# One string that orders 4,292 steps: the order of a gated recurrence and an MLP replaced by another order of the same instructions

## The chip, the core and the metric

The kernel runs on 1 core of one Trainium2 chip. The metric is device microseconds of one execution; three timed runs of the kernel before gave 839.09, 840.26 and 841.7 us, median 840.26 us. The trace comes from one profiled execution, whose span from the first to the last instruction is 837.2 us.

## What is computed

```
# q, k, v, a_re, a_im: (B, H, S, D) = (4, 8, 768, 48), float32
mag   = sqrt(a_re**2 + a_im**2)
scale = minimum(mag, 0.999) / (mag + 1e-6)          # a complex gate of modulus < 1
for t in range(S):                                  # state S: D x D complex, per batch and head
    S = gate[t] * S + k[t] (outer) v[t]
    y[t] = q[t] @ Re(S)
x = y, heads side by side: (B*S, H*D) = (3072, 384)
h = x @ w_in                                        # w_in: 384 x 2048, float64
g = maximum(h, 0) + alpha * minimum(h, 0)
out = g @ w_out                                     # w_out: 2048 x 384, float64; out: 3072 x 384
```

## The kernel before, in words

**The gates** (`gates`, lines 223 to 435). The recurrence is not run token by token. A prefix product of the gates gives each token a magnitude (a product over powers of two, "decays") and a phase ("rotation"). The work is cut into nine pieces: batch 0 in three (1, 2 and 3 chunks of 128 tokens), each of the other batches in two of 3 chunks. A piece loads `a_re` and `a_im` (L248), computes on ScalarE and VectorE (L254 to L311), builds the decays (L319) and writes them to DRAM (`decs`, L324), multiplies up the phases (L339, L341; the small ones on GpSimd) and writes those to DRAM (`phs`, L432).

**The units** (`unit`, from L646). One unit is one chunk of 128 tokens of one batch with all 8 heads: 24 units. `loads` fetches its q and k (L578, L580), its phases (`PP`, L586) and decays (`T`, L593). VectorE turns q and k by the phases (L662, L664) and then doubles the reach of the products level by level (L718, six levels); between these, ScalarE copies (L741, L757) feed small TensorE matmuls (L679), whose results are masked into `A` (L700 on ScalarE, L703 on VectorE). Further matmuls transpose k (L786), make the state of the chunk (L798), and sum the output y (L818, L842). The state passes from a unit to the next of its batch (L827, L830 on VectorE). y goes to DRAM (L861).

**The weights** (`to_f32`, from L490). w_in and w_out come as float64 words, in 16 loads (L492) into three regions of one buffer. Three ScalarE instructions (L508, L510, L512), one on GpSimd (L516) and two on VectorE (L518, L520) make each piece float32.

**The MLP** (`all_mlp`, L927). The tokens are handled in 14 groups of one or two chunks: sizes 1, 1, ten of 2, 1, 1. Once the units of a group have written y, its x is loaded (L874). Then for each of 16 blocks of 128 features: three matmuls (L890), Relu on ScalarE (L897), the slope on VectorE (L899), and, one or two blocks later, the matmul that adds the block to the output (L909). Each L890 or L909 call shows as two MATMUL records in the trace.

**What sets the order.** Every part is a Python generator. Its `yield`s cut it into steps: what stands between two yields (usually one instruction on one of VectorE, ScalarE, GpSimd, or a burst of TensorE matmuls, or one DMA issue on SyncE's queue) is one step. `Plan.run` (L96) walks through a string, `ORDER`, and for each letter advances the generator of that letter by one step:

```
    def run(self, order):
        for c in order:
            next(self.tasks[self.LETTERS.index(c)], None)
```

The letters are: A to I the nine pieces of the gates; J the loads of the units; K the rows of v for three of the levels (`half_rows`, L561); L the loads of v (L602 to L628); M the loads of the weights; N and O the making of w_in and w_out; P to Z and a to m the 24 units; n the loads of x; o the MLP. So the string alone fixes the program order of all instructions, and with it the order on each engine, since each engine runs its own instructions in program order, waiting at the first one whose inputs or buffer are not there. All DMAs are issued from SyncE's one queue, in the same way. Steps of one letter stay in their own order; only how the letters are mixed is free. `Ring` (L76) is left over from the making of the order: its `put` (L81) holds only `pass` and issues nothing.

Of the kernel before, what the change touches and what calls it, by code (L numbers as in the profile page):

```python
# [27 lines left out]


ORDER = (  # L30
    "AAAAAAAAAAAAAAAAAAAAAAAAAAMMMAAMMJBBBBAMBJNNNNAAAAAAAAAAAAABABNANAAAAAABAAAABBABBNNAABBMBBABBNAAAABB"
    "BBBKBAAKKBJNABAKBAKAKAKAKOKNKJKKKKAAAAKOBBBANAABKABOMAABMAAAAABABAAABAAOOOOOOOBNNOOBBNOONNBNMNNNBJJB"
    "BBBBOPJPONPPPPPNMNPPOOPOOOPPCCLLMMMLLLLBLLJBCBBBPBBBBBBBJJBBBBBBBBBBBBBPPPPPPNOBCCCPCPPPBBNKCKKKKKCK"
    "LLKLBBBBBOBLLPPPPPPPPBBBBBBBPCCCCCLCBBNCCJBBBBPPPOBOOOOCPPPPBCMJDDCCNCCOCOCPCJCNCOOCJJJCOCONNNNCCCPD"
    "DKCQCCCCCDDNCLLLLCQDCCQCCCCCCCCCCCOQLNLPPPPPPMQMQQQQPPPPJQQLODDQQQODJJOJJJJJJQQQDDQCQCCDCCQDCQRKCOKL"
    "CLLLLLLKnRRRQRQRQQQQQQQQQQRQRQQRCCCCCQCQCRCNNNDDCDDoDQooDoooLLLoooQoDMoLQooCDDDCoRCoCoCDoooooNRoNNCo"
    "CoKNCCCCLLLRRRoooooLLLLLLDRLRRQQCCCCCCCRKKRMKCCRRoQCDooCQQQQRRoRRQCCoooooCoCoDDDRRRRRRRRRRoDoRJORoDR"
    "oDOOOOODRJJEJNDoooooLLDRRRRoRRRRDoSoOooSDSooDLoooJoLLooSSDSEoooSJooDooonoSSoDoSSDNNNSLLENoDoSSSoooLN"
    "DLooooSDooRSSSEJoJooOOoooooSSSoJLESoTESSSSLoLLLoTSJoooJSSSJooJSoJJooooSSSSSSooDESSEKTKESSESSSSSSDSoo"
    "UDUooTTTDoDTDoDDDDDDKooDDDDoooooooTDTTTLEoEToooELLTTTTTooooLoooJoJoTTooooEoUTTTTTTTTooooooUUTToUTTLT"  # L40
    "EELLLLLLLLDDDDDDEEEDDDDDDDDLoooDDDDDDoTooTTTTooTLnLLLEEoooEUULLLLLLLKoTooooooEoLUEoooLoToDDUoTDooDUo"
    "DDDDooooooooUEoEEUUoEEEDTToTTTTTooToUoUoUoooUooDUooooDooooUUUUUUUUUoooooDDDUoDooUoUUooooEUUUUUUoDoEo"
    "oEoEoooJUJUUUUUEUEJEEJJoooooEJEoEJooooEoEooEUooEooEoooooVoooooooJEoVooVoVoooooVFFJJJooooUVJVVVFoEEoE"
    "EooEoEEEEEEVEVEnooJJVVELEEEoooooooLVoWWVVooLoLoLLFFVoooVVoooVWoLoEoooLoEooVLoWEWWVWoVEoVVVVoEoWLWLWE"
    "WLooEoFLVVVEVLoooVJJoVEoooVEJEJJWEEEEEoEFVVVVVVoWWVVVWFFFooELELoEooWFFFFFoooooLoWWLLLLLLWLoEoooooLEo"
    "EEEEoEoELLLoWWVVVVVVVEWVWWooooEoEooooJJEJooWoXWWWEFJWWEooooooWWoooooWWWWWWWWXWLLLWWWWWWWXFFooWoLLooL"
    "LXXXXoXooooXXXoJJJooooGXooooLXoFFFoGXXXXooooLXXooFoFooFoXYXoFXGonooooJJooLLGoYXXXooooXXXoXXoFLoLLFFF"
    "FYFooFoXYFoXoGYYYFYXYooFFooJJooFYoYooooooFKoJooJXXXXYXXLXXXXXGXXXXooFoXFooooFGoGooFFFFFFFFFFJJFJYYYY"
    "FooooYooYYooZoZZZoFooLoFLLLLooLLFLLFGLooooLooYYYYYLYLYoZYZZZZoooooKKKYKYooYooYooJooFFYFGKFFGZGJJGYYY"
    "YYYYYYYYLooLLoLFGKGoYYYYYYoZoKZoKooooooJoFLoFLFGoFGFFFoFFoFFFFFFFFFFoLLLZZZZnLZZZLooLLKooooLFFooooZo"  # L50
    "FZZooFFZFZFFoFoFJJFoJooFoFFooZZZJZJZoFZooooZZooZZZZZZZZZZZZFLLLFoaZZZZZaoooooooooooJaJJooaoGoooaaaaa"
    "ooooaoooooaoooGaaaaaaaaoooobooooGJGooLGoGGJGGaaaaaaaJJaLLLaGoGoooGoLLLLbbbbHHooooooaoooLoabLooaGGooG"
    "aaaaaaGaGaGHbbbHbGbHKbKGJaJaaooooooGGboooooooaoaaaGGaGoJoobbbboooGbbGbGGGGoGGGbcoooooooooLooLobLLLbL"
    "LLHJLbLJLcbLbboobooocoHobooooHHHooocobbbooocccccobbooLcnooLooooJJJHbbHHHbobbbbooLoHLLLHGccLLoLLLLLGL"
    "LHoGoooHoGooJGooHGboooooGoocGccGcGbGGGGbbGcGcGcGoooobobbobGJoooGGGGooGGGccccGGGGcoocccooLdccocoooodc"
    "ococccccccccccbbooJJLLGGGGGGGJJJGJcodcHcLLGococcHGGGoGoGooooooooLLoLoLoodooooodHGGdHoGodddddKKooHLLL"
    "LoKooHoooodoooddddJodLHLHoHddooJooHooHooddHooonodddHdoodddddooooHHHHHHHooooddIIoooodHHoddddJdddJddLH"
    "JdHdedddHHddeJJJoJJJJJJHooooooooooeooHoooooeeeeeeHeoeooooofooeooooofeeoeffeooeoooLLoooooJeoeooooooLe"
    "oeeeeeeffooogHHHHHHfHHHHHHHHHHHHHfHHHHHHHgHeeeeLLLLLLLLLLIKoooooeooeefeeeeeeeKeeeeeKeeeeHHooHooooofo"
    "ooJoHHHHfHJLLoLfoLHHLLLLoooLLooLffJJffIoILofLoLfofooooogoooogfgffffgfggfoffooooogggIoffooooooHHHHHHo"  # L60
    "HoooofIKooHHooofffffKKfngfHHofggggIIooKKLooooLLLLLLggLLLLgoLHoooggggggggoffffoffffooHofggfgoooooooHo"
    "ooooJJogooooLoooooIIgoooIJIIIIJoJgJJgggggggggohooIggggoIIoooooooIohhoogLLLLJJhhJJJoohoooooohhoooIooh"
    "hooohohoooohooonohoioIohhhhhohooiihoooooooooooJohiihiooIihIhhhIIIIhLoohooooKhoooohhLLoLLLLLILLIoIIIh"
    "oooiiihihhhhhhhhhhhhhhhhLoLhioooIooooooLLLLLooioiiioooiioioooIoooooiJiiiJooJJJLJJIIIIIIooooojoIoIooo"
    "ooIooIooojjIIIoIIIIoLIIoIIoIiijiiiiioooooooLojjLoLLoioLooioiIIIIiIIIIIIiIIIIIiiILLjLLLLLLLLojjjoioiI"
    "iioooojojooooojjioiIooIIiIIIIoILoojjjjojoooiILjjojiiioLLIIIIIIIIoIioooonjjjjjjjjooooIooIIooIooIooIoo"
    "oojooooojjjjjjjjjjjjjjjJJJJJjooooooojoooooJJJJoooookkLkoooooookoJooooookkoookkoookkoLojokokoookkkkko"
    "oJkoJJJJJkoooooookookkkkkkLLllLLoLLLLLoookkooLkLoooLkokookkkkkkkkkkkkkkklkokoooooooookLooooLllLllLLo"
    "nooooooololllJJloooooooJJooooooooLLoLollooomlollooolloooooooommmooooooomomolllolooooooommmmmoooLoLLL"
    "llllLooloooLmooommlmmoolloooooolollllllllllLlmllollloooooooooooooooooooomoooomoooooooooooooooooLLLLL"  # L70
    "LLooooooolooommmmmmoooooooooooomoooooooooooooomnoooooLLLLLooommmooooooomoommmmmmmmmmmmoooooooooomooo"
    "ommmoooooooooooonooooooooooooooooooooooooooooooooooooooooooooooooooooooooooooooooooooooooooooooooooo"
    "oooooooooooooooooooooooooooooooooooooooooooooooooooooooooooooooooooooooooooooooooooooooooooo")


# [26 lines left out]
def kernel(  # L102
# [83 lines left out]
    for h in (16, 32):  # L186
        by_row[h] = []
        for m in range(HC // h):
            t = next(column)
# [8 lines left out]
    def step(*args, **kwargs):  # L198
# [4 lines left out]
    R = {name: Ring(n) for name, n in dict(  # L203
        KQ=3, PP=1, T=2, V=1, WQ=2, W=1, run=1, St=3, xT=2, raw0=1, raw1=1, raw2=1, g0=0, g1=0, g2=0, ot=2, top=2,
        lv=2, misc=1, y=1, h=2, o=1).items()}
# [250 lines left out]
    def raw_done(name, f, e):  # L456

        i = 2 * f + (name == "out")
        for _ in range(6 if i >= NF - 3 else 1):
            R[("g" if i >= NF - 3 else "raw") + str(region(i))].put(e)  # L460
# [34 lines left out]
    def to_f32(dst, *key):  # L495

        n = 2 * DM
        ta = yield ACT(n + 100, ("raw", *key), takes=(R["top"],))
        raw = raws.pop(key)
        lo, hi = raw[:, :, :, 0], raw[:, :, :, 1]  # L500
        slot = slots.pop(0)
        top = tops[slot].rearrange("p (r e) -> p r e", r=dst.shape[1])
        top_u = top.bitcast(U32)

        def halfwords(z, dtype=U16):
            return z.rearrange("p r e -> p (r e)").bitcast(dtype)

        nc.scalar.activation(top, hi.bitcast(F32), AF.Abs)  # L508
        tl = yield ACT(n + 200)
        nc.scalar.activation(dst, lo, AF.Identity, scale=2.0 ** -51, bias=bias_two)  # L510
        tl = yield ACT(n + 100)
        nc.scalar.activation(halfwords(dst, BF16)[:, 1::2].rearrange("p (r e) -> p r e", r=dst.shape[1]), hi.bitcast(F32), AF.Sign, bias=bias_plus)  # L512
        raw_done(*key, tl)

        ta = yield POOL(1.4 * n, ta)
        nc.gpsimd.tensor_scalar(out=top, in0=top, scalar1=F64_SMALL, scalar2=None, op0=ALU.max)  # L516
        yield DVE(n // 2, ta)
        nc.vector.tensor_scalar(out=top_u, in0=top_u, scalar1=3, scalar2=None, op0=ALU.logical_shift_left)  # L518
        t = yield DVE(n, tl)
        nc.vector._custom_dve(ADD32_U16LIMBS, out=halfwords(dst), in0=halfwords(top), in1=halfwords(dst))  # L520
        slots.append(slot)
        return t

    def piece(dst, *key):
        if words:
            return (yield from to_f32(dst, *key))
        t = yield ACT(2 * DM, ("raw", *key))
        nc.scalar.copy(dst, raws[key])
        del raws[key]
        raw_done(*key, t)  # L530
        return t
# [470 lines left out]
```

## Time and profile before

| what | value |
| --- | --- |
| timed runs | 839.09, 840.26, 841.7 us |
| span of the profiled execution | 837.2 us |
| instructions | 26,824 |
| TensorE matmul busy | 696.3 us |
| VectorE (DVE) busy | 648.1 us |
| ScalarE (ACT) busy | 440.9 us |
| GpSimd (POOL) busy | 245.1 us |
| moved by DMA | 130.91 MB |

The page gives the busy time of each engine, then the span cut into 40 equal slices of 20.9 us, in which each digit is the busy share of an engine in tenths (9 is 90% or more). PEclk is the clock that TensorE was granted, in tenths of full speed. A row of a table by stretches gives, for a stretch of the span in us, the busy time of each engine with its instructions in brackets, the granted clock, the busy share of the 16 DMA engines, and what they moved in GB/s. A row of the waits reads: who waited (engine, what it writes, line), for whom, the time in total, how often, and the longest.

### The profile page before, as it was taken

What the parts mean: (1) busy time and instruction counts of PE and PEld (TensorE: products, weight loads), DVE (VectorE), ACT (ScalarE), POOL (GpSimd) and SP (SyncE); (2) the same over time, 40 slices, a digit from 0 to 9 for tenths busy, and PEclk for the clock granted to TensorE, in tenths of its full rate; (3) what the DMA queues carried; (4) which work ended last, traced back from release to release, by engine and by line L of the source; (5) the groups of instructions that cost most, each with busy time, mean ns of one, the idle gap of its engine ahead of it and who ended that gap; (6) DMA issues with size and microseconds to landing.
All of it is one profiled execution on the core that took longest, in us unless ns stands there. A gap on an engine that the chain in (4) does not pass through costs nothing.

```text
span 837.2 us, 26824 instructions
## 1 busy us (share of the span) xinstructions
PE 696.3 (83%) x11488; PEld 528.6 (63%) x11488; DVE 648.1 (77%) x953; ACT 440.9 (53%) x941; POOL 245.1 (29%) x352
## 2 busy tenths in 40 slices
PE   0002317768899999998999999999999999999998
PEld 0001316656777777776777777767777777777776
DVE  5988998989898998978998898796877856642112
ACT  7868876557645847473656544655443424232211
POOL 5376678817216400240134313500004300000000
PEclk9999757889999999999999999999999999999999
DMA  7695994696379468558854689457635493412100
GB/s 207 202 274 171 262 266 120 201 218 169 79 218 235 112 176 247 125 150 212 240 142 119 154 241 220 115 130 175 165 113 123 116 228 78 103 33 54 30 20 10
DMA packets 194174, 130.91 MB, mean 156 GB/s; under 512 B 74120, under 2 KB 185864, under 8 KB 194056
## 3 DMA queue, kind: packets, MB, share of 16 engines
q1 hardware_dynamic: 194056, 129.20, 58.7%
q8 instruction: 90, 1.47, 0.7%
q14 instruction: 28, 0.23, 0.1%
HBM read 100.82 MB, written 35.71 MB: 163 GB/s over the span
## 4 chain that ended last, share of the span: by engine, by line
PE 68%; DVE 12%; DMA 8%; ACT 5%; issue 3%; POOL 2%; SPq 2%; DVEq 0%; ACTq 0%; POOLq 0%
PE ps_h L890 27%; PE ps_o L909 26%; PE ps_lv L679 4%; PE ps_y L818 4%; DVE KQ L718 3%; PE ps_kv L798 3%; DMA T<-decs 3%; PE ps_y L842 2%; PE ps_kt L786 2%; DMA phs<-gate 2%; DVE gate L339 1%; DMA V<-in_v_dram 1%; DMA KQ<-in_k_dram 1%; DVE gate L341 1%; DMA St<-in_v_dram 1%
## 5 line engine op out<-in xcount | busy, mean ns | idle before, releaser
L890 PE MATMUL ps_h<-xT,w_in_sb 128*128 128x256 f32 (+1 forms) x1344 | 301.2, 356 | 3.0 <-issue 2.4
L909 PE MATMUL ps_o<-w_out_sb,g_sb 128*128 128x384 f32 x768 | 294.6, 497 | 10.7 <-DVE g_sb L899 8.3
L890 PEld LDWEIGHTS ps_h<-xT,w_in_sb 128*128 128x128 f32 x1344 | 234.1, 193 | 74.0 <-issue 4.3
L899 DVE SCALAR_TENSOR_TENSOR g_sb<-g_sb,al,ps_h 128x256 f32<-128x256 f32 (+1 forms) x224 | 97.5, 438 | 112.8 <-ACT g_sb L897 112.1
L909 PEld LDWEIGHTS ps_o<-w_out_sb,g_sb 128*128 128x128 f32 x768 | 137.7, 191 | 63.4 <-DVE g_sb L899 10.8
L718 DVE TENSOR_TENSOR KQ<-KQ,T 96x1024 f32<-96x1024 f32 x120 | 151.4, 1263 | 30.4 <-PE ps_lv L679 21.4
L897 ACT ACTIVATE g_sb<-ps_h 128x256 f32<-128x256 f32 (+1 forms) x224 | 78.7, 352 | 181.8 <-PE ps_h L890 181.1
L679 PE MATMUL ps_lv<-WQ 96*32 96x32 f32 x2304 | 34.5, 203 | 71.4 <-DVE WQ L662 55.1
L679 PEld LDWEIGHTS ps_lv<-WQ 96*32 96x32 f32 x2304 | 26.6, 115 | 93.1 <-DVE WQ L662 54.7
L339 POOL TENSOR_TENSOR gate<-gate 128x72 f32<-128x72 f32 (+1 forms) x56 | 40.0, 714 | 129.4 <-ACT gate L369 125.6
L741 ACT COPY WQ<-KQ 96x1024 f32<-96x1024 f32 x48 | 50.0, 1042 | 31.0 <-DVE KQ L718 30.7
L856 ACT COPY T<-ps_y 48x256 f32<-48x256 f32 x96 | 30.6, 365 | 46.8 <-PE ps_y L842 46.2
L757 ACT COPY W<-KQ 96x512 f32<-96x512 f32 x48 | 30.6, 638 | 45.7 <-DVE KQ L718 35.5
L516 POOL TENSOR_SCALAR top<-top 128x768 f32<-128x768 f32 x16 | 39.3, 2461 | 25.1 <-ACT top L508 17.1
L339 DVE TENSOR_TENSOR gate<-gate 128x576 f32<-128x576 f32 (+3 forms) x70 | 45.7, 653 | 1.2
L319 POOL TENSOR_TENSOR gate<-gate 128x72 f32<-128x72 f32 (+5 forms) x24 | 22.3, 929 | 76.6 <-DVE gate L319 74.3
L818 PE MATMUL ps_y<-A,VL 64*48 64x64 f32 x2304 | 43.5, 228 | 1.0 <-DMA VL<-vsc 0.7
L427 DVE TENSOR_TENSOR gate<-gate 128x1152 f32<-128x1152 f32 (+2 forms) x36 | 42.8, 1219 | 1.6 <-POOL gate L412 1.5
L679 PE MATMUL ps_lv<-KQ,W 96*32 96x32 f32 x1536 | 24.6, 205 | 23.4 <-ACT W L757 23.3
L818 PEld LDWEIGHTS ps_y<-A,VL 64*48 64x48 f32 x2304 | 41.6, 129 | 1.6 <-DMA VL<-vsc 0.9
L700 ACT ACTIVATE A<-ps_lv,columns 128x64 f32<-128x64 f32 x144 | 36.5, 334 | 9.6 <-PE ps_lv L679 9.5
L703 DVE TENSOR_TENSOR A<-ps_lv,mask 128x256 f32<-128x256 f32 x96 | 36.8, 412 | 0.0
(105 smaller groups left out, 925.3 us busy)
## 6 DMA issues: line engine op xcount, KB each, us to landing
T<-decs SPq DMA_DIRECT2D x48, 384.0 KB
PP<-phs SPq DMA_DIRECT2D x24, 387.0 KB
KQ<-in_q_dram SPq DMA_DIRECT2D x48, 192.0 KB
decs<-gate SPq DMA_DIRECT2D x7, 1152.0 KB
phs<-gate SPq DMA_DIRECT2D x14, 576.0 KB
KQ<-in_k_dram SPq DMA_DIRECT2D x40, 192.0 KB
vsc<-in_v_dram SPq DMA_DIRECT2D x48, 144.0 KB
VL<-vsc SPq DMA_DIRECT2D x24, 288.0 KB
```

Of the source, the lines that this page charges most:

```text
L339: on(4 * k).tensor_tensor(out=m, in0=w[:, 1::-1].unsqueeze(2).to_broadcast([P, 2, 2, k]), in1=pairs_of(u), op=ALU.mult)
L427: TT(out=m[:, a], in0=U5[:, 1 + a], in1=turned(off3, o)[:, a].unsqueeze(1).unsqueeze(3).to_broadcast([P, L // 2, nb, 2]), op=ALU.mult)
L516: nc.gpsimd.tensor_scalar(out=top, in0=top, scalar1=F64_SMALL, scalar2=None, op0=ALU.max)
L679: nc.tensor.matmul(t[64 * i + j:64 * i + j + HC // 2, p], lhsT=keys(n, g), rhs=queries(n, g), start=True, stop=True)
L703: nc.vector.tensor_tensor(out=a.rearrange("p n (g t) -> p n g t", g=2), in0=t.unsqueeze(2).to_broadcast(whole), in1=masks[name].rearrange( ...
L718: nc.vector.tensor_tensor(out=x, in0=x if x0 is None else x0, in1=m, op=ALU.mult)
L741: nc.scalar.copy(z.rearrange("p i n t -> p i (n t)").rearrange("p i (m h) -> p m i h", h=h), bass.AP(tensor=KQ.tensor, offset=KQ.offset + ...
L818: nc.tensor.matmul(o, lhsT=Vp[h][64 * i:64 * i + 64, s, e_ * D:(e_ + 1) * D], rhs=a, start=False, stop=False)
L890: nc.tensor.matmul(p, lhsT=w_in_sb[:, f // 2, kk, f % 2 * P:(f % 2 + 1) * P], rhs=x_of[m][:, kk], start=(kk == 0), stop=(kk == NK - 1))
L897: nc.scalar.activation(gt, p, AF.Relu, scale=-1.0)
L899: nc.vector.scalar_tensor_tensor(out=gt, in0=gt, scalar=al_1[:, f:f + 1], in1=p, op0=ALU.mult, op1=ALU.add)
L909: nc.tensor.matmul(sums[0], lhsT=gt[:, c * P:(c + 1) * P], rhs=w_out_sb[:, f], start=(f == 0), stop=(f == NF - 1))
```

## The change

The string is replaced by another one of the same length. Each letter occurs as often in the new string as in the old one, 1,552 times for the MLP, 49 times for most units. Besides, a line is added in `to_f32` that calls the empty `put`. The string has 43 lines; the first seven and the last two that differ are shown of each.

```diff
 ORDER = (
-    "AAAAAAAAAAAAAAAAAAAAAAAAAAMMMAAMMJBBBBAMBJNNNNAAAAAAAAAAAAABABNANAAAAAABAAAABBABBNNAABBMBBABBNAAAABB"
-    "BBBKBAAKKBJNABAKBAKAKAKAKOKNKJKKKKAAAAKOBBBANAABKABOMAABMAAAAABABAAABAAOOOOOOOBNNOOBBNOONNBNMNNNBJJB"
-    "BBBBOPJPONPPPPPNMNPPOOPOOOPPCCLLMMMLLLLBLLJBCBBBPBBBBBBBJJBBBBBBBBBBBBBPPPPPPNOBCCCPCPPPBBNKCKKKKKCK"
-    "LLKLBBBBBOBLLPPPPPPPPBBBBBBBPCCCCCLCBBNCCJBBBBPPPOBOOOOCPPPPBCMJDDCCNCCOCOCPCJCNCOOCJJJCOCONNNNCCCPD"
-    "DKCQCCCCCDDNCLLLLCQDCCQCCCCCCCCCCCOQLNLPPPPPPMQMQQQQPPPPJQQLODDQQQODJJOJJJJJJQQQDDQCQCCDCCQDCQRKCOKL"
-    "CLLLLLLKnRRRQRQRQQQQQQQQQQRQRQQRCCCCCQCQCRCNNNDDCDDoDQooDoooLLLoooQoDMoLQooCDDDCoRCoCoCDoooooNRoNNCo"
-    "CoKNCCCCLLLRRRoooooLLLLLLDRLRRQQCCCCCCCRKKRMKCCRRoQCDooCQQQQRRoRRQCCoooooCoCoDDDRRRRRRRRRRoDoRJORoDR"
...
-    "LLooooooolooommmmmmoooooooooooomoooooooooooooomnoooooLLLLLooommmooooooomoommmmmmmmmmmmoooooooooomooo"
-    "ommmoooooooooooonooooooooooooooooooooooooooooooooooooooooooooooooooooooooooooooooooooooooooooooooooo"
+    "AAAAAABBBMMAMAAMAMAAAAAJAAAJBAAKBAJAAAJAKABABMAAAANKBAAAABAAOAAAANAABABAABANBKLAKABBLAAMKAAAABAKNAAB"
+    "AAAABBLOOBAKAALAAAAAABBBBABMBAALALNNAABAABLAANBBABAAOANAAAANABABBOONBBMKBLBOBBBOOKBBBNKBOOJCOBNBBOOB"
+    "BNCNOONLBPCCNPPCKJBJOBOPNCBPBJBKCBPPBPBBNBBMCBBJCLBKKPBBKBPBPLBBLPNCBCPCBBJCBCMKKPBBNBCBMBPNBCCOCBPL"
+    "KPBPBPMBOBCNCBJBBOBMBNBOLBCBCCOBOKCKPPPCNNNCPPNONCPNCDOCPDPJCCJNCCNPPOCPPPONCPPOJPCCPPJCCCCDPCCNNPOL"
+    "DCPCPPNCDJPDCQMQCPPCQCPPDLDDPCDPJCCQQPCJPJMCnCCLQMDCDDDoDOQoOQJOCDDOQCDLNQCQCCJCOLoCODQOCOORKCLQRQQC"
+    "CLooCCCooCQRoCCooCoQoKoQLRCQoKooOooooRODDoOCoRMRoDLCQDQCCooQLoCQoCCDRoDKLDCCoJoRQQLoDRNooCQLDoooRoLQ"
+    "CJJQDCQDQoNoCQDKCNCQQQoQCRQCCQLoooQLRRQCCQRoQoDQoLMDNQLoQRLLQCLDoLLRDoRRJLQLoDQQQoLRRLDRoLDRoNJooooR"
...
+    "looolloooommoooLooolooooomoomlLoLoooooLLmnmoomooooomooooooomoooooooLoooooooooooLoooooooooooooLoooooL"
+    "mooooooommmmmommoooooooooooooomomooooooooooomomoooomomoooooooooooooooooooooooooommonoooooooooooooooo"
     "oooooooooooooooooooooooooooooooooooooooooooooooooooooooooooooooooooooooooooooooooooooooooooo")
...
         t = yield DVE(n, tl)
         nc.vector._custom_dve(ADD32_U16LIMBS, out=halfwords(dst), in0=halfwords(top), in1=halfwords(dst))
         slots.append(slot)
+        R["top"].put(t)
         return t
```

The change is described as found by a search over replays of traced durations. What the new string does can be read from it by counting what stands ahead of a step on its engine:

- At the head, the pieces A and B of the gates and the weights are mixed letter by letter instead of in runs. The loads of B stand right behind those of A.
- The first load of x (letter n) has 93 DMA issues ahead of it instead of 119; the first matmul of the MLP (letter o) stands at place 455 instead of 551 of the string.
- The making of the first w_in piece has 30 instead of 12 DMA issues ahead of it.
- In the middle and at the end, steps of units, gates and MLP alternate more finely; the last unit's last matmuls stand at place 4,132 instead of 4,083.

## Prediction

> **What bounds the kernel now.** I read the engines' totals and the slices first, then the chain, then stretches of 21 us, then the waits.
>
> ```profile
> PE 696.3 (83%) x11488; PEld 528.6 (63%) x11488; DVE 648.1 (77%) x953; ACT 440.9 (53%) x941; POOL 245.1 (29%) x352
> ...
> PE   0002317768899999998999999999999999999998
> ...
> DVE  5988998989898998978998898796877856642112
> ...
> PEclk9999757889999999999999999999999999999999
> ...
> PE 68%; DVE 12%; DMA 8%; ACT 5%; issue 3%; POOL 2%; SPq 2%; DVEq 0%; ACTq 0%; POOLq 0%
> ```
>
> TensorE is nearly full from the twelfth slice on and nearly empty in the first six. VectorE is the reverse: full from the second slice, slack only at the end. So it is a relay of two engines: VectorE makes what TensorE consumes, and what TensorE misses early it must do after VectorE has finished.
>
> ```profile
> 84.00:105.00 21.00, 7.73 (x228) 6.91 (x228) 20.57 (x27) 17.99 (x19) 13.59 (x8) 0.78 0.98 268
> 105.00:126.00 21.00, 3.94 (x192) 3.16 (x192) 20.26 (x25) 15.24 (x21) 15.15 (x16) 0.50 0.97 259
> 126.00:147.00 21.00, 16.41 (x338) 13.47 (x338) 17.83 (x25) 14.10 (x30) 17.74 (x19) 0.75 0.42 118
> ...
> 231.00:252.00 21.00, 21.00 (x311) 16.54 (x306) 20.27 (x30) 9.25 (x28) 1.80 (x2) 1.00 0.77 225
> ```
>
> After the stretch come TensorE, its weight loads, VectorE, ScalarE, GpSimd, the clock, the DMA share and GB/s. Up to 231 us TensorE is busy for 100 us, that is idle for 131; from 231 us on it is idle for only 10 us. VectorE is idle for 27 us of the first 231, 9.3 of them in the first 21. Around 84 to 126 us VectorE and the DMA engines (0.98, 0.97) are both full while TensorE starves.
>
> **The method.** Instructions and their durations stay; only places change. The code says what each letter's step issues. So I gave each instruction its traced time (to the next start where two overlap) and added, for each TensorE instruction in either string, the VectorE time that stands ahead of it and the TensorE time from it to the end. TensorE work that ran before 231 us, partly at a lower clock, got the mean of its line after that (L890 0.206 us a record, L909 0.333). That sum plus VectorE's idle time up to there is about the span, if VectorE feeds TensorE at that place. Largest sums, by VectorE time ahead:
>
> | VectorE ahead, us | 100-120 | 140-160 | 180-200 | 260-280 | 360-380 | 460-480 | 520-540 |
> | --- | --- | --- | --- | --- | --- | --- | --- |
> | old string | 791.0 | 801.4 | 804.2 | 797.2 | 788.5 | 777.2 | 762.3 |
> | new string | 790.0 | 802.1 | 799.0 | 800.5 | 797.1 | 788.7 | 778.7 |
>
> The old string has one peak, 804.2. VectorE's idle time there was 28.7 us, and 3.6 of it VectorE waited for TensorE itself (below), which is no delay of the relay: 804.2 + 25.1 = 829.3. The span is 837.2, so 7.9 us were lost later: 6.5 us of waits of TensorE after 217 us (4.6 of them "issue", waits that the profile lays to nothing), the rest about 1.5 us at half clock. The new string is flat: its peak is 2.1 us lower, but it has spent the slack that the old one had from 260 us on.
>
> **The change part by part.**
>
> *The head.* The writing of piece A's phases now has 25.7 us of VectorE ahead of it instead of 29.9, and unit 0's first step (L662) 37.9 instead of 39.2. But piece C's loads (two of 576 KB) are moved ahead of unit 0's decays (T) on the queue. At 263 KB per us of full DMA engines (129.20 MB in 58.7% of 837.2 us) they take 4.4 us. A's phases are out 4 us earlier, the rotation then lands near 47 us instead of 51, C's loads near 52, T near 55; in the old trace unit 0's L718 ran at 56.2. One step of C (L260, 1.28 us) now stands ahead of that L718. So unit 0 gains nothing, and C's loads go out some 6 us earlier (50.5 us before; now right behind the rotation's load, at 47.7 less 4); the cover is other gate work on VectorE, and without it the cost is those 4.4 us.
>
> *The first x.* The first x load has 93 DMA issues and 93.7 us of DMA time ahead of it instead of 119 and 108.6. The first L899 has 109.3 us of VectorE ahead instead of 116.4, so the MLP starts about 7 us earlier, near 130 us. But block 16 of the first group has 162.9 against 164.1: the last weights bind (last w_in piece: 156.8 against 158.0 us of VectorE). An early start fills TensorE's hole, and the sums hold what remains: 1 us at 120, 5 us at 180 to 200.
>
> *Queues and other engines.* The same sums with the DMA engines in VectorE's place peak at 786 instead of 793 us, with ScalarE at 773.6 instead of 775.9, with GpSimd at 761.9 instead of 754.3. DMA gains 7 us, and GpSimd's 7.6 us are covered by 40 us of distance to VectorE's peak.
>
> *VectorE's idle time* is not in any old row for the new string, so I bound it. Below: the first 10.1 us and the 3.0 us of gaps that remain by 155 us of work when the 12.0 us of waits in the profile's list for 10 to 180 us are taken from the old 25.1; above: all of the old. Of that list:
> ```profile
> DVE g_sb L899 <- ACT g_sb L897: 2.5, 3, 1.0
> DVE KQ L718 <- ACT top L508: 1.7, 1, 1.7
> DVE WQ L662 <- DMA V<-in_v_dram: 1.7, 1, 1.7
> DVE St L726 <- DMA St<-in_v_dram: 1.5, 1, 1.5
> ...
> DVE KQ L718 <- DMA T<-decs: 0.5, 1, 0.5
> DVE WQ L662 <- DMA PP<-phs: 0.5, 1, 0.5
> ```
>
> L899 waits on L897, which waits on TensorE's L890 (181.1 us over the run): that, and L718 waiting on L679, is VectorE waiting for TensorE. By 180, 300, 410, 520 and 597 us these waits add up to 2.9, 7.6, 15.6, 22.9 and 37.0 us. Taking them out of the old idle time, the new sums become 802.1 + 25.1 - 2.9 = 824.3 near 155 us of VectorE, 800.5 + 33.8 - 7.6 = 826.7 at 265, 797.1 + 46.2 - 15.6 = 827.7 at 370, 788.7 + 58.7 - 22.9 = 824.5 at 469, 778.7 + 74.7 - 37.0 = 816.4 at 522. The highest, **827.7**, counts. From it I take 4.2 us, the four DMA waits shown, since the DMA work ahead is less; this is a choice between 0 and the 14.6 us that VectorE waited on DMA, ScalarE and GpSimd between 10 and 410 us. I add the 4.6 us of "issue" waits, which no order touches. The added `put` has `pass` as its body: nothing.
>
> **Sum.** 827.7 - 4.2 + 4.6 = 828.1 us of span. The median of the timed runs, 840.26, stands 3.0 above the profiled span: 828.1 + 3.0 = **831 us**, 1.1% faster.
>
> *The clock.* TensorE's granted clock was 0.78, 0.50 and 0.75 from 84 to 147 us, while it was 37%, 19% and 78% busy, and 1.00 from 231 us. The sum takes the same work at full clock and lets VectorE bind. The Trainium skill, "TensorE: Matmul & The Clock Gate", Part 1, says that TensorE drops to half rate after an idle window of about 3.4 us and rises after a busy one; by it, an MLP that starts as scattered single blocks would run at half rate for longer. The low stretch in the trace agrees in direction.
>
> **The rivals.**
> 1. *All waits come back.* 827.7 plus the old 7.9 us of later loss: 835.6, with 3.0 it is 838.6 us, no measurable change. For it: the flat sums leave no slack to absorb a late wait.
> 2. *The slack is what was needed: slower.* At 460 to 480 us of VectorE the new string has 11.5 us more ahead than the old. If VectorE's waits for TensorE do not shrink when more of its work stands ahead, the old idle time of 58.7 us stays: 788.7 + 58.7 = 847.4, with 3.0 it is 850 us. It decides once VectorE's idle time there exceeds 48.5 us (837.2 - 788.7). Against it: waits for TensorE shrink when VectorE arrives later.
> 3. *The small waits go.* At the lower bound of VectorE's idle time the sum is 802.1 + 10.1 + 3.0 = 815.2, and with 3.0 around the span 818 us. For it: DMA, the releaser of a third of the listed waits, has less ahead. Against it: each piece of work moved forward moves another back.
> 4. *The low clock lasts.* If TensorE ran at 0.5 from 126 to 210 us, where it did about 55 us of full-clock work in 84 us, that would take 110, 26 us more. Half of it, since half that work has no slack: 828.1 + 13 + 3.0 = 844 us. For it: the row of 105 to 126 us. Against it: the MLP's work lies denser there than the units' alone.
> 5. *The string does nothing.* Excluded: only 1,100 of 4,292 letters stand where they stood.
>
> **How the numbers follow.** Forecast (825 to 837) 0.43; rival 1, 0.14; rival 2, 0.20; rival 3, 0.18; rival 4, 0.05. This measurement tells changes over about 0.3% (2.5 us) from none. Faster: 0.43 + 0.18 = 0.61; same: 0.14; slower: 0.25. The range runs from rival 3's 818 to rival 2's 850; I leave about a tenth beyond each end. The forecast's own range is 825 to 837.
>
> **What would show it.** Right: the sixth slice (105 to 126 us) has more than 3.94 us of TensorE; the first x load issues before 120 us (128.4 before) and the first L899 before 132 (137.2 before); VectorE's idle time at 192 us of its work is below 28.7; DMA waits of VectorE in the first 180 us fall below 4.2 us; TensorE idles 10 us or less once full. Wrong: VectorE idles over 48 us before 469 us of its work is done, or TensorE shows fresh idle time after 300 us (waits of L890 on x, of L909 on L899, of L679 on L757), or the clock stays at 0.5 past 147 us. The prediction would fail above all if new head-of-queue waits on SyncE's queue hold the T or x loads.

## The result, and the profile after

The changed kernel takes 871.98 us (median of four runs, 866.46 to 873.94), the kernel before, run beside it, 840.98 (839.09 to 845.73): a ratio of 1.0361, with a 95% interval of 1.0313 to 1.0409. It is 3.6% slower, outside the range of 818 to 850. The profiled execution has a span of 870.5 us, 33.3 more than before. Lines below 521 carry a number one higher (L818 is now L819).

First the page of the changed kernel: totals, TensorE's slices, the chain.

```profile
PE 708.3 (81%) x11488; PEld 536.7 (62%) x11488; DVE 645.7 (74%) x953; ACT 439.5 (50%) x941; POOL 263.1 (30%) x352
...
PE   0000336879898999999999999999999999999998
...
PE 68%; DVE 11%; POOL 9%; issue 5%; ACT 3%; DMA 3%; SPq 0%; DVEq 0%; ACTq 0%; POOLq 0%
```

The instructions are the same and VectorE's busy time is too. But TensorE works 12.0 us longer on the same matmuls, and in the chain "issue", time in which the engine waited for nothing that the profile shows, went from 3% to 5%. Now the stretches shown for the kernel before:

```profile
84.00:105.00 21.00, 7.38 (x218) 6.34 (x219) 20.18 (x28) 15.42 (x24) 11.24 (x6) 1.00 0.98 285
105.00:126.00 21.00, 6.29 (x152) 5.23 (x151) 19.49 (x21) 15.57 (x19) 17.91 (x14) 1.00 0.79 216
126.00:147.00 21.00, 13.76 (x208) 10.61 (x209) 17.26 (x24) 13.16 (x26) 19.10 (x25) 1.00 0.48 128
231.00:252.00 21.00, 20.71 (x386) 15.51 (x384) 19.97 (x29) 10.40 (x21) 0.77 (x3) 1.00 0.57 176
```

In the first two rows the clock of 1.00 is no reading: this trace has no record of the clock before 140.2 us (more at rival 4 below). Seen like this, the early stretches are not what went wrong: 105 to 126 us has more busy time of TensorE (6.29 for 3.94 us), and up to 231 us TensorE is idle 134 us, 3 more than before. A run below nevertheless lays 13 us of the loss to the head. After 231 us TensorE is idle for 28 us where it was 10. Its waits there, all that are listed, first of the changed kernel, then of the kernel before (waiter, releaser, total, times, longest):

```profile
PE ps_y L819 <- issue: 15.2, 9, 3.4
PE ps_lv L680 <- issue: 4.3, 3, 1.6
PE ps_y L843 <- issue: 3.4, 3, 1.8
PE ps_lv L680 <- ACT W L758: 0.6, 2, 0.3
```

```profile
PE ps_h L890 <- issue: 2.4, 2, 1.3
PE ps_o L909 <- issue: 2.2, 1, 2.2
PE ps_y L818 <- DMA VL<-vsc: 0.7, 1, 0.7
PE ps_h L890 <- DVE g_sb L899: 0.6, 2, 0.4
PE ps_lv L679 <- ACT W L757: 0.4, 2, 0.3
```

So "issue" grew from 4.7 to 22.8 us, while all other idle time of TensorE after 231 us stayed as it was (5.4 and 5.3 us). The groups of TensorE name the place; first two of the changed kernel, then the one row of the kernel before that answers to the first (busy, mean ns of one, idle time before them and its releaser):

```profile
L819 PE MATMUL ps_y<-A,VL 64*48 64x64 f32 x2304 | 46.0, 229 | 24.6 <-issue 23.8
L843 PE MATMUL ps_y<-KQ,St 96*48 96x64 f32 x768 | 30.4, 236 | 3.4 <-issue 3.4
```

```profile
L818 PE MATMUL ps_y<-A,VL 64*48 64x64 f32 x2304 | 43.5, 228 | 1.0 <-DMA VL<-vsc 0.7 <-issue 0.2
```

Over all groups TensorE's "issue" time went from 5.8 to 31.5 us. These waits are few and long. In the timeline of the changed kernel (start, duration, operation, count, and in brackets the idle time before) a typical one looks like this:

```profile
410.13 1.07 PE L819 MATMUL ps_y<-A,VL 64*48 64x64 f32 x64
413.24 1.00 PE L819 MATMUL ps_y<-A,VL 64*48 64x64 f32 x28 [2.04 <-issue]
```

A run of 92 equal matmuls, with all its inputs there, stops for 2.04 us in the middle. Counting TensorE's instructions from the start (each MATMUL record is two, a weight load and the matmul, and a semaphore record counts too; most float32 matmul calls make two MATMUL records), this gap stands at number 192 or 193 modulo 256. So do all 13 gaps over 1 us that TensorE has after 231 us, and the 3 of the kernel before. Near each gap there is one packet of 16,384 bytes on queue q8, which the page calls "instruction" (90 packets, 1.47 MB). So I read the gaps as TensorE waiting for its next block of 256 instructions. The traces bear this out: the twelve kernels of this study that do the whole computation have 103 "issue" gaps over 0.5 us after 90 us, 102 of them at number 192 or 193 and one at 194, and in each of them TensorE went on 1.1 to 1.7 us after the end of the one such packet that had started since the block began. The kernel before has 4 such gaps over 0.5 us after its first 90 us, 5.7 us in all; the changed one 16, with 31.0 us.

Why more of them? The string before breaks the units' small matmuls with blocks of the MLP. The new one issues a unit's tail in one go: runs of at least 224 small MATMUL records without the MLP went from 4 to 14. Such a run has 450 and more instructions, so it often holds a whole block of 256, and that block is done in 1.7 to 2.7 us. In the kernel before, 4 blocks after 200 us last under 3.5 us, in the changed one 16; one of the 4 and 13 of the 16 end in a gap over 0.5 us.

### The profile page after: what moved, and what is told of

Same layout as the page of the kernel before. It is cut to its first block, busy times and chain, and to the rows that moved or that the text cites. A ratio compares the mean times of both kernels' runs of the same rounds, so it can differ in the third digit from the quotient of the medians.

```text
span 870.5 us, 26819 instructions
## 1 busy us (share of the span) xinstructions
PE 708.3 (81%) x11488; PEld 536.7 (62%) x11488; DVE 645.7 (74%) x953; ACT 439.5 (50%) x941; POOL 263.1 (30%) x352
## 3 DMA queue, kind: packets, MB, share of 16 engines
q8 instruction: 90, 1.47, 0.7%
## 4 chain that ended last, share of the span: by engine, by line
PE 68%; DVE 11%; POOL 9%; issue 5%; ACT 3%; DMA 3%; SPq 0%; DVEq 0%; ACTq 0%; POOLq 0%
PE ps_o L910 26%; PE ps_h L891 26%; PE ps_lv L680 5%; PE ps_y L819 4%; PE ps_y L843 3%; PE ps_kv L799 2%; POOL gate L339 2%; POOL top L516 2%; DVE gate L339 2%; DVE KQ L719 2%; PE ps_kt L787 2%; DVE gate L427 2%; POOL gate L341 1%; POOL run L341 1%; DVE gate L341 1%
## 5 line engine op out<-in xcount | busy, mean ns | idle before, releaser
L891 PE MATMUL ps_h<-xT,w_in_sb 128*128 128x256 f32 (+1 forms) x1344 | 304.2, 361 | 5.8 <-DMA xT<-ysc 5.7
L910 PE MATMUL ps_o<-w_out_sb,g_sb 128*128 128x384 f32 x768 | 299.0, 505 | 8.0 <-DVE g_sb L900 6.8
L891 PEld LDWEIGHTS ps_h<-xT,w_in_sb 128*128 128x128 f32 x1344 | 239.2, 197 | 78.3 <-issue 6.1
L898 ACT ACTIVATE g_sb<-ps_h 128x256 f32<-128x256 f32 (+1 forms) x224 | 79.1, 353 | 238.7 <-PE ps_h L891 237.9
L910 PEld LDWEIGHTS ps_o<-w_out_sb,g_sb 128*128 128x128 f32 x768 | 138.5, 193 | 60.7 <-DVE g_sb L900 8.8
L719 DVE TENSOR_TENSOR KQ<-KQ,T 96x1024 f32<-96x1024 f32 x120 | 148.6, 1239 | 36.9 <-PE ps_lv L680 25.4
L680 PE MATMUL ps_lv<-WQ 96*32 96x32 f32 x2304 | 34.6, 204 | 72.5 <-DVE WQ L663 52.5
L339 POOL TENSOR_TENSOR gate<-gate 128x72 f32<-128x72 f32 (+1 forms) x56 | 35.7, 637 | 165.8 <-ACT gate L369 162.2
L680 PEld LDWEIGHTS ps_lv<-WQ 96*32 96x32 f32 x2304 | 26.4, 116 | 95.1 <-DVE WQ L663 52.8
L819 PE MATMUL ps_y<-A,VL 64*48 64x64 f32 x2304 | 46.0, 229 | 24.6 <-issue 23.8
L742 ACT COPY WQ<-KQ 96x1024 f32<-96x1024 f32 x48 | 50.0, 1042 | 17.8 <-DVE KQ L719 17.6
L819 PEld LDWEIGHTS ps_y<-A,VL 64*48 64x48 f32 x2304 | 42.3, 129 | 27.1 <-issue 26.2
L857 ACT COPY T<-ps_y 48x256 f32<-48x256 f32 x96 | 31.5, 365 | 42.8 <-PE ps_y L843 42.2
L701 ACT ACTIVATE A<-ps_lv,columns 128x64 f32<-128x64 f32 x144 | 39.4, 335 | 12.5 <-PE ps_lv L680 12.5
L680 PE MATMUL ps_lv<-KQ,W 96*32 96x32 f32 x1536 | 24.7, 205 | 25.2 <-ACT W L758 22.3
L339 POOL TENSOR_TENSOR gate<-run,runs 128x12 f32<-128x12 f32 x46 | 28.5, 620 | 42.7 <-ACT runs L369 39.5
```

Source lines behind the costliest of these rows:

```text
L339: on(4 * k).tensor_tensor(out=m, in0=w[:, 1::-1].unsqueeze(2).to_broadcast([P, 2, 2, k]), in1=pairs_of(u), op=ALU.mult)
L680: nc.tensor.matmul(t[64 * i + j:64 * i + j + HC // 2, p], lhsT=keys(n, g), rhs=queries(n, g), start=True, stop=True)
L701: nc.scalar.activation(a[:, :, cols], t[:, :, at:at + name], AF.Copy, scale=s)
L719: nc.vector.tensor_tensor(out=x, in0=x if x0 is None else x0, in1=m, op=ALU.mult)
L742: nc.scalar.copy(z.rearrange("p i n t -> p i (n t)").rearrange("p i (m h) -> p m i h", h=h), bass.AP(tensor=KQ.tensor, offset=KQ.offset + ...
L819: nc.tensor.matmul(o, lhsT=Vp[h][64 * i:64 * i + 64, s, e_ * D:(e_ + 1) * D], rhs=a, start=False, stop=False)
```

## The experiments

Four theories. **A**: TensorE stands whenever a block of 256 instructions is done faster than the next one is fetched, some 3.5 us. **B**: the loss is in the order's own waits, the slack that the new string has spent (rival 2 above), and the gaps fill time that would be lost anyway. **C**: the fetch is late only because data fills the DMA engines. **D**: the head of the string makes the loss. (Where an expectation uses a letter otherwise, it says so.)

A can be tested without any change of order. Cut into blocks at another phase, the records of the kernel before would have up to 19 short blocks instead of 4: the old string sits at a lucky phase. A few tiny matmuls ahead of everything, while TensorE waits for its first inputs, shift the phase and nothing else.

**Shift by 136 instructions**

```diff
+    pad = ps.tile([P, HP, D2], F32, tag="misc", name="ps_kt")
+    for _ in range(68):
+        nc.tensor.matmul(pad[0:D, 0, 0:D], lhsT=nothing[0:64], rhs=nothing[0:64], start=True, stop=True)
```

> The old string, with 68 tiny bf16 matmuls (136 TensorE instructions, results unused) ahead of everything, while TensorE is idle anyway. Theory A (instruction blocks): TensorE gets its instructions in blocks of 256 and stalls when one block runs out in under about 3.6 us; by adding traced durations per block the old string has 4 such blocks, and with all instructions shifted by 136 it would have 19, short by 26 us together. Adding some 5 us for the lower clock after stalls: 841 + 31 = 872 us (860 to 880), with about 15 or more waits of kind issue on TensorE. Theory B (the order spends VectorE's slack): nothing in the order changed, 841 us, within 2. Theory C (DMA traffic delays the fetches): traffic unchanged, 841 us, within 2.

Measured: 883.72 us, a ratio of 1.0515 [1.0467, 1.0562]. The waits of TensorE after 231 us (waiter, releaser, total, times, longest):

```profile
PE ps_y L818 <- issue: 22.8, 13, 4.8
PE ps_y L842 <- issue: 8.0, 2, 4.8
PE ps_lv L679 <- issue: 4.7, 3, 2.1
```

No letter of the order was moved, and the old string became slower than the new one. 19 gaps with 37.0 us instead of 4 with 5.7, all at number 192 or 193 modulo 256. B and C, which expected 841 us, cannot make that. A's size was too small: it cost 43 us, not 31, and the time lies just above A's range.

**Shift by 240 instructions**

```diff
-    for _ in range(68):
+    for _ in range(120):
```

> The same with 120 tiny matmuls (240 instructions). Theory A: the shift of 240 leaves 3 short blocks, 1.6 us short together instead of 3.0: 838 to 842 us. Theories B and C: 841 us, within 2. If it is slower by 5 us or more, the padding itself costs time and the other padded run can't be read as the blocks' doing.

Measured: 837.29 us, 0.9954 [0.9932, 0.9977]. 120 extra matmuls cost nothing; two gaps are left, 2.3 us. The time lies just under A's range of 838 to 842. It is the fastest kernel of the study, faster than both strings as they stand.

**Shift by 24 instructions**, a dose

```diff
-    for _ in range(68):
+    for _ in range(12):
```

> The old string with 12 tiny matmuls (24 TensorE instructions) ahead of everything: a dose. By the records of the kernel before, cut into blocks of 256 instructions 24 later, 11 blocks instead of 4 last less than 3.6 us and lack 14.6 us instead of 3.0; for a shift of 136 the same sum gave 30.1, and that run cost 43 us over the kernel before, 1.6 us for each microsecond that lacked more. Theory A (a block must last about 3.6 us, or TensorE stands at its end): 839.5 + 11.6 x 1.6 = 858 us (850 to 866), with stalls at instruction 192 modulo 256 near 11 places. Theory B (the padding's cost has nothing to do with the phase): 839 to 841 us, as with 240 instructions.

Measured: 852.3 us, 1.0162 [1.0131, 1.0193], with 8 gaps over 0.5 us and 15.5 us. A holds: inside its range, though below its number. Per microsecond of gaps added, the shifts of 24 and 136 cost 1.3 and 1.4 us.

**The new string, shifted by 136**: the lines of the first experiment, put into the changed kernel

```diff
+    for _ in range(68):
+        nc.tensor.matmul(pad[0:D, 0, 0:D], lhsT=nothing[0:64], rhs=nothing[0:64], start=True, stop=True)
```

> The new string with the same 68 tiny matmuls (136 TensorE instructions) that cost the old one 43 us. By the records of the kernel after, cut 136 instructions later, 16 blocks instead of 18 last less than 3.6 us and lack 24.6 us instead of 19.8: the new string has no lucky phase to lose. Theory A: 872 + 4.8 x 1.6 = 880 us (872 to 886), with the stalls at other times than in the kernel after, again at instruction 192 modulo 256. Theory B (136 instructions ahead of everything cost some 40 us in any order): 910 to 916 us.

Measured: 863.8 us, 1.0294 [1.0271, 1.0318]: faster than the unshifted new string, where I expected it a little slower (872 to 886); A's range is missed. So 136 instructions cost nothing by themselves, and B's 910 is out. There are still 14 gaps, but shorter, 17.6 us in all. My count of what short blocks lack assumed one fetch time for all of them, and the last section shows that it isn't one; that this is the whole of the miss is not shown.

**Small matmuls by themselves.** Blocks of small matmuls alone, with loads, with writes and without DMA, then runs of 48 small ones broken by big ones:

```diff
+        small(640)
+        big(24)
+        load(60)
+        big(24)
+        small(640)
...
+        for n in (4, 8, 12, 16):
+            for _ in range(8):
+                small(48)
+                big(n)
```

> TensorE alone; everything of the computation is left out, and the output is a constant. 640 small float32 matmuls (64 x 48 by 64) back to back with no DMA, the same during 60 loads of 192 KB, then groups of 48 small ones with 4, 8, 12 and 16 of the 128 x 256 matmuls between them. Theory A: the small ones (about 16 ns a record) use up 256 instructions in about 2 us, so after the first one or two blocks there is a wait of 1 to 2.5 us at the end of every block, with DMA or without, and one block takes 3.3 to 4.5 us; with 8 or more big ones between, no waits. Theory C (DMA traffic): waits only in the part with loads. If neither part shows waits, the cause isn't the rate of instructions.

Measured: span 325.4 us. The loads ran during the first section of small matmuls, since SyncE's queue is not tied to TensorE; the writes of the output reached into the second. Timeline in the second section, the first row beside the writes and the second with the DMA idle:

```profile
94.94 2.00 PE L54 MATMUL ps_y<-a 64*48 64x64 f32 x128 [2.00 <-issue]
...
117.58 2.00 PE L54 MATMUL ps_y<-a 64*48 64x64 f32 x128 [1.73 <-issue]
...
132.42 1.56 PE L54 MATMUL ps_y<-a 64*48 64x64 f32 x96
133.90 1.99 PE L59 MATMUL ps_h<-x,w 128*128 128x256 f32 x8
```

Exactly 128 MATMUL records, 256 instructions, and a stop after each. From one block's start to the next it takes 3.45 to 3.7 us with the DMA idle, 4.0 to 4.3 beside the writes and 4.8 to 5.65 beside the loads, longer there than A expected (3.3 to 4.5). The matmuls of a block take 2.0 us of it (2.8 to 3.7 in the first section, where the clock was low for much of the time). With big matmuls between (last two rows) there is no stop. So A needs no data traffic, and C is partly true: traffic makes the fetch longer.

**Breaking the bursts with MLP steps**, in the new string and in the old one:

```diff
-    "TEEUEEToEEoLJooUooLoELooooEoLLUoDooooDoEooDoUUTooToToTLLULTooooToDUTUoTUTLLTUoLoLooJoEoUTooEEooEoooU"
+    "UUUoDoTEEUEETEELJULoELooooEoLLUoDooooDoEooDoUUTooToToTLLULTooooToDUTUoTUTLLTUoLoLooJoEoUTooEEooEoooU"
...
```

> The new string, in which MLP steps are pulled forward by a few places into the units' tails wherever the sum of durations gives a 256-instruction block of TensorE under 4 us; everything else keeps its order. Theory A: the 16 short blocks (22 us short) become 1 (0.7 us); with the low clock that followed the stalls about 28 us go: 872 - 28 = 844 us (838 to 852), with under 5 us of issue waits on TensorE. Theory B: VectorE gets the MLP's steps earlier, so it is as much ahead as before or a little less: 862 to 874 us. Theory C: 866 to 874 us.

> The old string treated in the same way (67 pulls of a few places). Theory A: the 4 short blocks go, 4.7 us of stalls: 835 to 839 us. Theory B: 841 us or up to 5 us slower, since VectorE meets MLP steps that still wait for TensorE. Theory C: 841 us, within 2.

Measured: 879.44 us, 1.0457 [1.042, 1.0494], and 857.93 us, 1.021 [1.0168, 1.0252]. Both missed the ranges of all three theories. After 231 us the gaps fell to 3 (3.0 us) and 1 (1.1 us), but the idle time of TensorE that is not "issue" rose there to 22.1 us (5.3 in the new string) and 17.6 us (5.4 in the old one); one row of each:

```profile
PE ps_lv L680 <- ACT W L758: 8.0, 8, 2.0
```

```profile
PE ps_lv L679 <- DVE KQ L718: 3.7, 2, 2.9
```

Moving MLP steps also moved their Relu on ScalarE and slope on VectorE ahead of the units' steps, and the units' matmuls (L680, L679) then waited for those two engines. B has a point: neither order has slack to give there.

**Only the steps that TensorE alone does**, so that the order on all other engines stays as the new string has it:

```diff
-    "LSDDooKooLSoORSoSEooDSLDOoJoSoSLoRoSLEoDKoLSLDSSoJDEDLSJoJSoDSLSoooooToTooSoSDDoSoDoETSTSTJToDDSDSSE"
+    "LSDDooKooLSoORSoSEooDSLDOoJoSoSLoRoSLEoDKoLSLDSSoJDEDLSJoJSoDSLSoooooToTooSSDDSDETSTSTJooooToDDSDSSE"
...
```

> The new string, in which only MLP steps that issue TensorE matmuls and nothing else are moved by a few places into or out of units' bursts, so that the order on VectorE, ScalarE, GpSimd and the DMA queue stays exactly that of the new string. By the sums the blocks of 256 TensorE instructions that last under 3.6 us fall from 16 (22 us short) to 9 (5 us short). Theory A (instruction blocks): issue waits of TensorE fall from 32 us to some 10, and with the clock after them the time falls from 872 to 849 us (842 to 857). Theory B (the order spends VectorE's slack; the stalls only hide other waits): other waits of TensorE take their place, 866 to 874 us.

Measured: 862.8 us, 1.0275 [1.022, 1.033], between the two theories. Gaps after 231 us fell from 22.3 to 8.2 us, and 9 us of time went with them; L680 and L799 waited 7.3 us for ScalarE there, where it had been 0.6 us. These waits are read from the profiled execution, which was the slowest of the four (868.0 us; the fastest took 856.8).

**Head of one, body of the other.** The first 1,200 letters (up to about 250 us on TensorE) of one string, then the remaining steps in the other's order. First the old head with the new body:

```diff
-    "AAAAAABBBMMAMAAMAMAAAAAJAAAJBAAKBAJAAAJAKABABMAAAANKBAAAABAAOAAAANAABABAABANBKLAKABBLAAMKAAAABAKNAAB"
+    "AAAAAAAAAAAAAAAAAAAAAAAAAAMMMAAMMJBBBBAMBJNNNNAAAAAAAAAAAAABABNANAAAAAABAAAABBABBNNAABBMBBABBNAAAABB"
...
```

> The first 1,200 letters of the old string (until about 240 us), then the rest in the order of the new one. By 250 us the new kernel had lost 6 us more of TensorE's time than the old; the other 27 of 33 us it lost later. Theory A: the body's blocks lie as in the new kernel, so 841 + 27 = 868 us (862 to 873), with 20 us or more of issue waits after 231 us. Theory D (the head, where the new string mixes everything, made the loss, and it is only paid later): 841 to 847 us.

Measured: 858.44 us, 1.0212 [1.0178, 1.0245], 13 gaps after 231 us with 21.1 us. It is faster than A's range (862 to 873), and D's 841 to 847 is out: most of the loss stays with the new body. Then the new head with the old body; in the changed kernel's string 30 lines differ, from the thirteenth on:

```diff
-    "UoUUUooEoTLUEooUUJEUUoEUooooooEUoFUoVUUUEoUUUUEVFoUUoJUVUUUEFVJooooVoooVoVVEFooEEVJVooEEoVEooVVoFVJo"
+    "KKLTUUUUUUUUUUUUUUUUUUUUUUUUEUEEEJEJEEJEEooEUooEooEoooooVoooooooJEoVooVoVoooooVFFJJJooooUVJVVVFoEEoE"
...
```

> The first 1,200 letters of the new string, then the rest in the order of the old one. Theory A: the body's blocks lie as in the old kernel, 2 to 4 of them short: 841 + 6 = 847 us (842 to 852). Theory D: 862 to 872 us.

Measured: 852.56 us, 1.0153 [1.0114, 1.0193]. 19.2 and 13.3 us against the kernel before add up to 32.5, about the whole loss (31.0). The head's part lies just beyond what A allowed (842 to 852). In this run TensorE has lost 13 us against the kernel before by 300 us and no more after. Up to 231 us it has three gaps of 7.9 us and a wait of 5.8 us for the first x.

**The head at another phase.** 192 instructions ahead of everything, 48 more at 243 us, so that the old body again runs at 240:

```diff
+            if (m, f, kk) == (4, 5, 0):
+                for _ in range(24):
+                    nc.tensor.matmul(p[0:D, 0:D], lhsT=nothing[0:64], rhs=nothing[0:64], start=True, stop=True)
...
+    for _ in range(96):
+        nc.tensor.matmul(pad[0:D, 0, 0:D], lhsT=nothing[0:64], rhs=nothing[0:64], start=True, stop=True)
```

> The first 1,200 letters in the new order, the rest in the old (852.6 us without padding, with 7.9 us of stalls in the head), now with 96 tiny matmuls (192 TensorE instructions) ahead of everything and 24 more (48) at about 243 us, so that the head runs at the phase at which its blocks lack least, and the old body at the phase of 240, which costs nothing. By the records of that run the head's blocks lack 1.6 us instead of 3.1 by a bound of 4 us, and the blocks that ended in stalls of 2.7 and 4.3 us are no longer whole inside a burst or last 2.8 us. Theory A, the head's 13 us are mostly stalls: 852.6 - 6.3 + 0.7 = 847 us (844 to 849.5). Theory D, the head's loss is in the waits of the later units (the first unit's end at 109 us instead of 98, the x load's wait), and stalls only fill time that those waits would take: 851 to 855 us, with the stalls gone and longer waits on VectorE or ScalarE.

Measured: 855.62 us, 1.019 [1.015, 1.023]. That is just above D's range, but the test failed, for the gaps did not go: 6.4 us of them in the head, and in the body, where the phase was meant to cost nothing, 5.6 us after 231 us (1.3 in the run without padding). Among TensorE's waits from 160 to 260 us there is still this one, beginning at 176.7 us:

```profile
PE ps_lv L680 <- issue: 4.5, 1, 4.5
```

The burst there is so long that 192 instructions later another whole block, of 2.8 us, lies in it. How the head's 13 us divide between gaps, the x wait and the later units stays open.

## Why the prediction was wrong

- **The step that failed**: "I add the 4.6 us of "issue" waits, which no order touches." The order does touch them: how densely it packs small matmuls, and where its bursts fall among blocks of 256 instructions, sets them. In the stretch that the term was taken from, after 217 us, they were 22.8 us in the changed kernel instead of 4.6; over the whole run they went from 5.8 to 31.5 us. With 22.8 for 4.6 the sum would give a span of 846.3 and a time of 849; with all 25.7 us that came on top, 853.8 and 857. So this one term explains 18 to 26 us of the error of 41 us, and not all of it.
- **A second step** that failed is the bound on VectorE's idle time, "above: all of the old". At 469 us of VectorE's work it is 75.0 us, above the old 58.7 (more below).
- **Where the 33.3 us of span are.** From 231 us on, the changed kernel needs 33.3 us more. Of these, 18.1 are more idle time of TensorE, and "issue" accounts for all of it. The other 15.2 are more busy time: some 8 of them are half clock (17.1 us of it after 231 us against 0.9; an estimate that counts half of the difference as lost), and the remaining 7 are work that was still undone at 231 us.
- **What comes with it**: the clock. The granted clock fell to half for 3.4 to 6.8 us with the gaps of 3.37, 1.82, 2.04 and 1.91 us that began at 263, 300, 411 and 523 us (the windows at 266, 304, 413 and 526), while the kernel before had no half clock from 218 us to its last microsecond. Over the whole run L891 and L910 took 0.52 and 0.89 us where half clock is on record and 0.36 and 0.49 where 1.00 is, and they were busy 7.4 of the 12.0 us longer. In the old string shifted by 136 the clock was at half for 30.7 us after 231 us, and TensorE was busy 14.1 us longer there than unshifted: that is what its gaps cost beyond their own length. The Trainium skill, "TensorE: Matmul & The Clock Gate", Part 1, says that half rate follows at least one idle window of about 3.4 us; here the windows have that length, but an idle time of 1.82 us was enough. Nor does the gap's length alone decide: in the kernel before one of 2.23 us was followed by none. All clock records of these three kernels but the last of each are whole multiples of 3.41 us; the 3.41 us just ahead of the four windows were idle for 88, 53, 60 and 56%, while the gap of 2.23 us fell across two such steps, 24 and 42% idle.
- **The method.** The sums of durations left out a cost that hangs on neither engine's work but on the count of instructions. Even so the flat sums may have said something true: in the new string, 14 us fewer gaps after 231 us bought 9 us (only TensorE's steps moved), and 13 us fewer in the shifted one bought 8, while in the old string every added microsecond cost 1.3 to 1.4. In the first of these, waits for ScalarE took the place of part of the rest; in the second it is not shown what did.
- **The head** came as worked out at first: A's phases were out 2.7 us earlier (4 forecast), the rotation's load at 42.7 us instead of 47.7, C's loads at 43.2 instead of 50.5. But unit 0's L718 was 3.4 us later, not level, and unit 1 started at 109.9 instead of 98.5 us, which I had not foreseen.
- **The first x** was asked for at 116.9 us (128.4 before): right. The first L899 was at 133.8 (137.2), not before 132, and the 16th at 194.1, 4 us later than before.
- **DMA waits of VectorE** from 10 to 180 us fell from 4.2 to 1.7 us (3.4 with one ahead of 10 us): right, and worth nothing here.
- **VectorE's idle time** at 192 us of its work is 36.5 us, not below 28.7, and at 469 us it is 75.0. That meets the condition of rival 2 (over 48.5), yet its mechanism is not what the runs show. VectorE's idle time is largely this wait, in the changed kernel:

```profile
DVE g_sb L900 <- ACT g_sb L898: 148.8, 105, 6.6
```

It was 112.1 us before, and L898 waits for TensorE's L891. I read this as VectorE idling because TensorE stands; TensorE stood in the shifted old string too, with VectorE's order untouched.
- **Rival 4** (the low clock lasts) was right in part. Where a trace has no record yet, the views show 1.00, and the records begin at 92.2 us before and 140.2 us after. The same six matmuls of L891, start and duration, ahead of that and just behind it:

```profile
122.17 1.65 PE L891 MATMUL ps_h<-xT,w_in_sb 128*128 128x128 f32 x6 [5.75 <-DMA xT<-ysc]
142.10 0.94 PE L891 MATMUL ps_h<-xT,w_in_sb 128*128 128x128 f32 x6
```

So TensorE still ran slowly up to 140.2 us, as it did up to 136.6 us in the kernel before (where L890's matmuls took 0.42 us each at half clock, as L891's here at 122 us). Between 126 and 231 us that makes 38 us of low clock instead of 28, which can have cost some 5 us of work by then (an estimate: half of the difference). For the same reason the prediction's 0.78 from 84 to 105 us is too high: up to 92.2 us it counts 1.00 without a record. **Rivals 1 and 3** (838.6 and 818) fell with the result; **rival 5** was out, as said.

## What to carry to other kernels

A long idle time that the profile lays to "issue", in the middle of equal matmuls, should be counted out: if it always falls at the same number modulo 256, it is instruction fetch, and any order with bursts of small matmuls longer than a block is exposed to it. A model of durations and waits does not see it, so an order found on such a model may pack exactly what must not be packed. Before comparing two orders, shift each by a few dozen instructions: the old one here spans 837 to 884 us by phase alone.

## What the runs showed of the hardware

A block of 256 TensorE instructions needs one packet of 16 KB, which itself takes about 1.0 us. When the 256 instructions ahead of a gap over 0.5 us had taken less than 2.6 us (60 such blocks, in eight kernels), it mattered how busy the DMA engines were during the block. At a share under 0.4 (25 blocks) the packet started 0.9 us after the block did, and the block with its gap took 3.4 us (medians; 2.7 to 4.1). At 0.92 or more (13 blocks) the packet started after 2.5 us, and block and gap took 5.0 us (3.5 to 7.0). Two stretches of the changed kernel, queues with packets, MB and share, the first (172 to 181 us) around the gap of 4.45 us at 176 us, the second (551 to 557 us) around that of 1.51 us at 556 us:

```profile
q1 hardware_dynamic: 2781, 2.49, 112.6%
q8 instruction: 1, 0.02, 0.8%
```

```profile
q1 hardware_dynamic: 98, 0.04, 3.2%
q8 instruction: 1, 0.02, 1.0%
```

In the first the data queue fills the engines by itself (packets overlap, so the share passes 100%), and the one packet of instructions started 4.9 us after its block did; in the second the engines are nearly free and it started after 1.2 us. This is a comparison across gaps, with the loads and writes beside the small matmuls above as its only experiment. The Trainium skill, "Runtime: NRT & Kernel Launch", section "Instruction fetch mechanics", also has blocks of 16 KiB or 256 instructions, and calls the cost of crossing one "mostly hidden". For TensorE the runs show where that ends. In the twelve kernels after 200 us, 63 of 71 blocks done in under 3.0 us ended in a gap over 0.5 us, 5 of 23 done in 3.0 to 3.5 us, and 17 of 823 longer ones, 14 of them at a DMA share of 0.77 or more.
